# Four down row tiles behind the last product of a gate and up unit, in groups 2 to 6

## The chip, the core and the metric

The kernel runs on one core of a Trainium2 chip. The metric is the time of one execution on the device, in microseconds (us). Of the core's engines this case speaks of TensorE (PE, with its weight loads shown apart as PEld), VectorE (DVE), ScalarE (ACT), GpSimd (POOL), and SyncE (SP), which here issues DMAs only. GpSimd issues DMAs too, and does small adds.

## What is computed

The kernel computes a Fourier mixing layer, gated by a feed-forward layer, on x of 2048 rows and 448 columns in fp32:

```python
def _A_ref(x, dft_seq_re, dft_seq_im, dft_hid_re, dft_hid_im):
    a = jnp.einsum("bsd,ed->bse", x, dft_hid_re)
    b = jnp.einsum("bsd,ed->bse", x, dft_hid_im)
    y = jnp.einsum("ts,bse->bte", dft_seq_re, a) - jnp.einsum("ts,bse->bte", dft_seq_im, b)
    return y

def _B_ref(x, w_gate, w_up, w_down):
    return (_gelu(x @ w_gate) * (x @ w_up)) @ w_down

x = A_x
xn = _layernorm(x, axis=-1)
s = _A_ref(xn, A_dft_seq_re, A_dft_seq_im, A_dft_hid_re, A_dft_hid_im)
g = _silu(_B_ref(xn, B_w_gate, B_w_up, B_w_down))
return x + s * g
```

w_gate and w_up are 448 x 1792, w_down is 1792 x 448. The change lies in `_B_ref`.

## The kernel before

The 1792 feed-forward columns are 14 tiles of 128, taken in pairs: `GROUPS` has seven groups of two tiles, counted from 0. The 2048 rows are four chunks of 512. Group 0 computes gate and up directly. Groups 1 to 6 use a scheme with fewer products, in the function `strassen` (line 482): one call, a **unit**, makes gate and up for one tile of 128 columns and two chunks. A group has four units (tile 0 or 1, chunk pair 0 or 1), in the order of the loop at line 851; `gi` is the group, `bi` the unit in it, 0 to 3, and the text calls them first to fourth.

fp32 numbers are kept as a high and a low part, and a product is two or three matmuls of 128 x 128 weights against 512 columns (`three`, `two`, lines 470 and 477). A unit has 39 of them, in seven sums of 5 or 6 matmuls, in four accumulators in PSUM, `x1` to `x4`, in this order: x1, x2, x3, x4, then x1, x3 and x4 are opened again and added to. Between a first and a second filling another engine must have read the accumulator: ScalarE copies x1 (L500), VectorE adds x2, x3 and x4 into two temporaries (L505, L512, L516). After the second fillings ScalarE takes a GELU of x1 (L521), VectorE adds and multiplies (L525, L526), ScalarE writes the high part of the first product tile `hs` (L528), VectorE its low part (L530); then x4 is read (L534) and its GELU taken (L535). The unit's second product tile is finished in the next unit: L539 (VectorE, multiply), L541 (ScalarE, high part) and L544 (VectorE, low part) are passed on as `late` and called behind that unit's x1 and x2.

**Down** takes the product tiles of a group and a chunk and makes four row tiles of 128 rows (`down_one`, line 441): six matmuls of 448 columns into a PSUM tile `po`, then a ScalarE copy (L457) into a staging tile `po_out`. Behind the fourth copy GpSimd issues the DMA `gs<-po_out` (L462), which adds the staged tile to `gs` in device memory. The row tiles wait in a list, `dq`; `send` takes the next and emits it. `strassen` calls `dn[0]` to `dn[3]` at four places: behind x2, behind x4, behind the second filling of x3, and behind the second filling of x4. A unit in groups 2 to 6 emits four row tiles of work that earlier units made, one at each place.

Each engine takes its instructions in the order in which they are written; there is no scheduler. `preps` are steps of weight preparation that are written between the same places: a first and a fourth unit split the next weights (`prep_s`: ScalarE L356, VectorE L358 and L362), a third unit the down weights (`prep_d`: L384, L385), a second unit none. In groups 2 to 5 the second and the third unit begin with `sums_s` (line 332): ten GpSimd adds of 128 columns, L338 to L347, on the raw weights of the next group. They stand in GpSimd's queue behind the last unit's `gs` DMA, and in some units also behind two DMAs `sums<-ca` that `sum_step` issues there (L809).

Of the kernel before, what the change touches and what calls it, by code (L numbers as in the profile page):

```python
# [45 lines left out]
def fnet_geglu(ctx: ExitStack, tc: tile.TileContext, x, ca, ct, cp, et, wgu, wd, out):  # L46
# [209 lines left out]
    def t_places(p):  # L256
        if not t_lo:
            t_lo.append(sb.tile([P, 4096], FR, name="t_lo", tag="y"))
        h = [a_x[2 * p + 1][:, o : o + 512] for o in (0, 512, 2048, 2560)]
        l = [t_lo[0][:, 2048 * p + 512 * i :][:, :512] for i in range(4)]  # L260
        t_hl[p][0] = list(zip(h, l))

        def one(i):
            side, k = SPOT[i]
            split(h[i], l[i], xfk(2 * p + side, k))

        return one

    def v_places(p):
        v = sb.tile([P, 4096], FR, name=f"t_v{p}", tag=f"v{p}")  # L270
        vt[p] = v
        hl = []
        for side, k in SPOT:
            hl.append([v[:, 2048 * side + 512 * (k + 2 * a) :][:, :512] for a in range(2)])
        t_hl[p][1] = hl

        def one(i):
            side, k = SPOT[i]
            h, l = hl[i]
            n = 64 if i == 3 else P  # L280
            split(h[:n], l[:n], xfk(2 * p + side, k + 2)[:n])
            if i == 3:
                for a in (h, l):
                    nc.sync.dma_start(a[64:].bitcast(F32), a[:64].bitcast(F32))

        return one
# [12 lines left out]
    def load_s(f, i):  # L299
        raw = a_r[i]  # L300
        nc.sync.dma_start(raw[:, :1280], wgu[f].rearrange("p b f -> p (b f)"))
        return raw
# [29 lines left out]
    def sums_s(raw, eng):  # L332


        g2d, u2d, g3, u3, u0, g0, g1, u1, g2, u2, s3, s2, s4, s7, s6 = [
            raw[:, i * P : (i + 1) * P] for i in range(15)
        ]
        eng.tensor_sub(s3, g0, u0)  # L338
        eng.tensor_sub(s7, g2, u2)
        eng.tensor_add(u0, u0, u1)  # L340
        eng.tensor_add(u2[:64], u2[:64], u3[:64])
        eng.tensor_sub(s2, u0, g0)
        eng.tensor_sub(s6, u2, g2)
        eng.tensor_sub(s4, g1, s2)
        eng.tensor_sub(u2d, g2d, u2d)
        eng.tensor_add(u2d, u2d, g3)
        eng.tensor_sub(u2d, u2d, u3)  # L347
# [26 lines left out]
    def load_d(grp, at):  # L374
        rv = at[:, : 2 * D].rearrange("p (f d) -> p f d", f=2)
        nc.sync.dma_start(
            rv, wd[grp[0] * P : (grp[0] + 2) * P, :].rearrange("(f p) d -> p f d", p=P)
        )
        return rv
# [61 lines left out]
    def down_one(gi, c, wdn, kk):  # L441
        if gi > 0 and kk >= 2:
            po = tp_tile(f"po{gi}_{c}_{kk}")
        else:
            po = o_tile(f"po{gi}_{c}_{kk}")
        n = 0
        for i, f in enumerate(GROUPS[gi]):
            hs = hs_of[f, c]
            for a, b in ((0, 0), (0, 1), (1, 0)):
                nc.tensor.matmul(  # L450
                    po[:, :D], hs[:, a, kk * P : (kk + 1) * P], wdn[b][:, i],
                    start=n == 0, stop=n == 5,
                )
                n += 1
        if kk == 0:
            out_[0] = stage(c)
        nc.scalar.activation(out_[0][:, kk], po[:, :D], AF.Copy)  # L457
        if kk == 3:
            if gi == 0:
                nc.sync.dma_start(gv[:, 4 * c : 4 * c + 4], out_[0])  # L460
            else:
                nc.gpsimd.dma_start(gv[:, 4 * c : 4 * c + 4], out_[0], accum_op=ALU.add)  # L462
# [88 lines left out]
    with tc.manual_schedule():  # L551
# [156 lines left out]
        def fetch(p):  # L708
            nc.sync.dma_start(x_half(p), xp[p])
# [105 lines left out]
        def send():  # L815
            if dq:
                down_one(*dq.pop(0))

        nop = lambda: None
# [3 lines left out]
        def e_load(b):  # L823
            e_raw[b] = a_r[0][:, 960 * (b % 2) :][:, : 2 * D]
            nc.sync.dma_start(e_raw[b], et[b].rearrange("p r d -> p (r d)"))
# [17 lines left out]
        for gi in range(1, len(GROUPS)):  # L843
            grp = GROUPS[gi]
            nxt = GROUPS[gi + 1] if gi + 1 < len(GROUPS) else None
            ws = nws
            if gi > 1:
                wdn = nwdn
            nws, n_raw = [None, None], {}
            sides = (0, 0, 1, 1) if gi % 2 else (1, 1, 0, 0)  # L850
            for bi, (i, p) in enumerate(zip((0, 1, 1, 0), sides)):
                preps = [[], [], [], []]
                if gi == 1 and bi == 0:
                    tsp, vsp = t_places(1), v_places(1)
                    preps[0].append(lambda: (comb1.pop(0)(), vsp(3)))
                    preps[2].append(lambda: comb1.pop(0)())
                    preps[3].append(lambda: comb1.pop(0)())
                if gi == 1 and bi == 1:
                    comb1.pop(0)()
                    for n, f, k in ((0, vsp, 1), (1, tsp, 1), (2, tsp, 2), (3, vsp, 2), (3, tsp, 0)):  # L860
                        preps[n].append(lambda f=f, k=k: f(k))
                if gi == 1 and bi == 2:
                    vsp(0)
                    tsp(3)
                if bi == 0:
                    if gi == 1:
                        sums_s(s_raw2, nc.gpsimd)
                        n_raw[-1] = s_raw2
                    else:
                        n_raw[-1] = last_raw  # L870
                    ws[1], steps = prep_s(nw, n_raw[-1])
                    preps[1].append(steps[0])
                    preps[2].append(steps[1])
                    if nxt and gi > 1:
                        n_raw[0] = load_s(nxt[0], 0)
                    elif not nxt:
                        e_load(0)
                        e_load(1)
                elif bi == 1:
                    if nxt:  # L880
                        n_raw[1] = load_s(nxt[1], 1)
                        if gi > 1:
                            n_raw["d"] = load_d(nxt, a_s)
                            sums_s(n_raw[0], nc.gpsimd)
                        else:
                            wdn, steps = prep_d(grp, draw)
                            preps[1] += steps
                    else:
                        E_IN[0] = sb.tile([P, 1920], FR, name="e0", tag="r1")
                        preps[1].append(lambda: (e_split(0, E_IN[0]), e_load(2)))  # L890
                elif bi == 2:
                    if nxt:
                        if gi == 1:
                            n_raw["d"] = load_d(nxt, a_s)
                            n_raw[0] = load_s(nxt[0], 0)
                            sums_s(n_raw[0], nc.gpsimd)
                        sums_s(n_raw[1], nc.gpsimd)
                        nwdn, steps = prep_d(nxt, n_raw["d"])
                        preps[1].append(steps[0])
                        preps[2].append(steps[1])  # L900
                    else:
                        fetch(1)
                        E_IN[1] = sb.tile([P, 4 * D], FR, name="e1", tag="d1")
                        E_IN[2] = sb.tile([P, 2240], FR, name="e2", tag="sp")
                        preps[1].append(lambda: (e_split(1, E_IN[1]), e_load(3)))
                        preps[3].append(lambda: e_split(2, E_IN[2]))
                else:
                    if nxt:
                        nws[0], steps = prep_s(nw, n_raw[0])
                        preps[1].append(steps[0])  # L910
                        preps[2].append(steps[1])
                    else:
                        preps[1].append(lambda: e_split(3, vt[1][:, 7 * D :]))
                dn = [send] * 4
                if gi == 1 and bi < 2:
                    dn = [nop, send, nop, send]
                run = [lambda q=q: [f() for f in q] for q in preps]
                late = strassen(grp[i], p, ws[i], late, dn, run)
                sum_step(4 * gi + bi - 4)
                if bi % 2:  # L920
                    dq += [(gi, c, wdn, kk) for c in (2 * p, 2 * p + 1) for kk in range(4)]
            nw = 1 - nw
            if nxt:
                last_raw = n_raw[1]
# [484 lines left out]
```

## Time and profile before

| | us |
|---|---|
| Median of 3 runs | 769.03 (768.9 to 769.06) |
| The profiled execution | 769.27 |
| Its span in the trace | 767.5 |
| PE busy | 761.3 |
| DVE busy | 544.4 |
| ACT busy | 366.6 |
| POOL busy | 179.9 |

The span is what the trace covers from first to last instruction; the execution is 1.8 us longer. Times in rows are us from the span's start. In the chain of work that ended last, a row is a stretch of one engine and line; the chain's places are up to 0.2 us later than the start of the same matmuls in the timeline, since a row of a matmul overlaps the next. Groups 2 to 6 run from 122 to 398 us.

### The profile page before, as it was taken

The numbers are of one execution on the slowest core, as the hardware profiler recorded it, in microseconds if no ns is written. First come the engines' busy times: TensorE is split into PE (matmuls) and PEld (weight loads), VectorE is DVE, ScalarE is ACT, GpSimd is POOL, SyncE is SP. The second block draws the span as 40 slices with busy tenths as digits, with TensorE's granted clock in tenths as the row PEclk, the third lists the DMA queues.
The fourth block names the chain that finished last, engine by engine and source line by source line (L and its number), as shares of the span: only waits on it lengthen the run. The fifth ranks groups of instructions, "written<-read, shape, count | busy, mean of one in ns | idle before, by whom it ended". The sixth has DMA issues, their size and how long they took to land.

```text
span 767.5 us, 11360 instructions
## 1 busy us (share of the span) xinstructions
PE 761.3 (99%) x4054; PEld 686.2 (89%) x4054; DVE 544.4 (71%) x946; ACT 366.6 (48%) x547; POOL 179.9 (23%) x303
## 2 busy tenths in 40 slices
PE   8999999999999999999999999999999999999998
PEld 7988888888888888888889999999999999999997
DVE  7879877555556556455452777978888797979787
ACT  5975554444444344344444585534444444434341
POOL 2204043430501511501011001223222222323130
PEclk9999999999999999999999999999999999999999
DMA  8234458994959968774979981959696969688794
GB/s 298 91 120 150 145 203 172 263 186 104 266 107 252 272 117 225 172 157 84 257 218 240 372 346 54 325 170 334 210 354 205 346 202 343 211 304 268 256 312 153
DMA packets 61513, 170.04 MB, mean 222 GB/s; under 512 B 7440, under 2 KB 40080, under 8 KB 60560
## 3 DMA queue, kind: packets, MB, share of 16 engines
q0 software_dynamic: 13728, 61.02, 35.0%
q1 hardware_dynamic: 34272, 82.48, 30.5%
q10 hardware_dynamic: 13456, 25.81, 9.2%
q8 instruction: 32, 0.52, 0.3%
q14 instruction: 25, 0.20, 0.1%
HBM read 127.21 MB, written 70.91 MB: 258 GB/s over the span
## 4 chain that ended last, share of the span: by engine, by line
PE 99%; DVE 0%; issue 0%; DVEq 0%
PE x L473 24%; PE p L1173 22%; PE po L450 18%; PE p L1176 10%; PE ab L984 9%; PE x L480 4%; PE gu L396 4%; PE py L1188 1%; PE py L1190 1%; PE py L1189 1%; PE gu L599 1%; PE pt L198 1%; PE warm L573 1%; PE p L1206 0%; PE gu L585 0%
## 5 line engine op out<-in xcount | busy, mean ns | idle before, releaser
L473 PE MATMUL x<-xt,w 128*128 128x512 f32 x480 | 149.6, 392 | 0.0
L473 PEld LDWEIGHTS x<-xt,w 128*128 128x128 f32 x480 | 90.1, 188 | 16.3 <-DVE tmp L512 0.7
L457 ACT ACTIVATE po_out<-po 128x448 f32<-128x448 f32 x112 | 60.2, 537 | 81.7 <-PE po L450 79.5
L450 PE MATMUL po<-wd0h,hs 128*128 128x448 f32 x256 | 81.7, 366 | 0.0
L462 POOL DMA_DIRECT2D gs<-po_out x24 | 21.4, 893 | 218.7 <-ACT po_out L457 213.7
L984 PE MATMUL ab<-e,xt 128*128 128x448 f32 x288 | 68.8, 365 | 0.0
L450 PE MATMUL po<-wd,hs 128*128 128x448 f32 x288 | 66.0, 365 | 0.0
L473 PE MATMUL x<-t_v,w 128*128 128x512 f32 x216 | 60.8, 390 | 0.0
L450 PEld LDWEIGHTS po<-wd,hs 128*128 128x128 f32 x288 | 54.1, 188 | 6.7
L984 PEld LDWEIGHTS ab<-e,xt 128*128 128x128 f32 x288 | 54.1, 188 | 4.3
L450 PEld LDWEIGHTS po<-wd0h,hs 128*128 128x128 f32 x256 | 48.1, 188 | 4.9
L473 PEld LDWEIGHTS x<-t_v,w 128*128 128x128 f32 x216 | 40.6, 188 | 8.7
L1064 POOL DMA_DIRECT2D raw<-sums x45 | 24.8, 552 | 94.9 <-DVE xt L143 56.6
L450 PE MATMUL po<-wd0l,hs 128*128 128x448 f32 x128 | 46.9, 367 | 0.0
L142 ACT ACTIVATE e<-raw 128x896 fp32r<-128x896 f32 (+1 forms) x30 | 27.6, 921 | 38.6 <-DVE raw L1071 27.8
L528 ACT ACTIVATE hs<-tmp 128x512 fp32r<-128x512 f32 x24 | 15.2, 634 | 54.6 <-DVE tmp L526 54.6
L473 PE MATMUL x<-t_lo,w 128*128 128x512 f32 x96 | 37.4, 389 | 0.0
L142 ACT ACTIVATE e<-tmp 128x896 fp32r<-128x896 f32 (+1 forms) x22 | 19.7, 896 | 35.7 <-DVE tmp L1071 28.6
L1173 PE MATMUL p<-t_v,wd0l 128*128 128x448 f32 x112 | 36.4, 374 | 0.0
L1173 PE MATMUL p<-w,e 128*128 128x448 f32 x112 | 36.4, 374 | 0.0
L1064 POOL DMA_DIRECT2D tmp<-sums x39 | 21.5, 552 | 59.9 <-DVE xt L143 37.2
L358 DVE TENSOR_TENSOR w<-raw,w 128x512 fp32r<-128x512 f32 (+1 forms) x24 | 21.3, 888 | 18.3 <-ACT w L356 18.3
(374 smaller groups left out, 2017.6 us busy)
## 6 DMA issues: line engine op xcount, KB each, us to landing
gs<-po_out POOLq DMA_DIRECT2D x24, 896.0 KB, 7.8
sums<-ca SPq DMA_DIRECT2D x16, 896.0 KB, 11.2
sums<-ca POOLq DMA_DIRECT2D x16, 896.0 KB, 14.5
t_v<-td ACTq DMA_DIRECT2D x24, 448.0 KB, 5.8
w<-td ACTq DMA_DIRECT2D x24, 448.0 KB, 7.5
raw<-ct SPq DMA_DIRECT2D x45, 192.0 KB, 4.2
raw<-wgu SPq DMA_DIRECT2D x12, 640.0 KB, 5.9
tmp<-ct SPq DMA_DIRECT2D x39, 192.0 KB, 4.6
```

The source lines that it names most:

```text
L142: nc.scalar.activation(h, src, AF.Copy)
L358: nc.vector.tensor_sub(w[:, 1408 + lo : 1408 + b], raw[:, P + lo : P + b], hw[:, lo:b].bitcast(F32))
L396: nc.tensor.matmul(ps[:, cols], a, xt[:, cols], start=n == 0, stop=n == len(mm) - 1)
L450: nc.tensor.matmul(po[:, :D], hs[:, a, kk * P : (kk + 1) * P], wdn[b][:, i], start=n == 0, stop=n == 5,)
L457: nc.scalar.activation(out_[0][:, kk], po[:, :D], AF.Copy)
L462: nc.gpsimd.dma_start(gv[:, 4 * c : 4 * c + 4], out_[0], accum_op=ALU.add)
L473: nc.tensor.matmul(ps, a[i], b[j], start=first and n == 0, stop=n == 2, skip_group_check=True)
L480: nc.tensor.matmul(ps, a[0], xt, start=False, stop=True, skip_group_check=True)
L984: nc.tensor.matmul(p[:, :D], a, b, start=n == 0, stop=n == len(mm) - 1)
L1064: nc.gpsimd.dma_start(v[:, 4 * P : 6 * P], sums[j][:, KS.index(k)])
L1173: nc.tensor.matmul(ps[q][:, :D], h, v, start=u % UN == 0, stop=False, skip_group_check=True)
L1176: nc.tensor.matmul(ps[q][:, :HD], l, v[:, :HD], start=False, stop=u % UN == NS - 1, skip_group_check=True,)
```

## The change

The list of calls `dn` is filled differently. In group 1 nothing changes. In groups 2 to 6 the first three places are empty, and the fourth, behind the second filling of x4, emits four row tiles in a row.

```diff
-                dn = [send] * 4
-                if gi == 1 and bi < 2:
-                    dn = [nop, send, nop, send]
+                dn = [nop, nop, nop, lambda: [send() for _ in range(4)]]
+                if gi == 1:
+                    dn = [nop, send, nop, send] if bi < 2 else [send] * 4
```

The same row tiles are emitted in the same units, with the same matmuls, copies and DMAs. The order on GpSimd and SyncE is the same as before; on PE, ACT and DVE it moves, on DVE only in the numbers of the names.

On PE in the first unit of group 2, from the last products of x3's first filling to its second filling, before (the names are out<-in; `x3_4_1` is accumulator x3 of column tile 4 and chunk pair 1, `po1_2_1` a down row tile of group 1, `w` the weights, `xt`, `t_lo` and `t_v` parts of the input):

```order
L473 MATMUL x3_4_1_1252<-t_v1_822,w_73 128x512 x3
L473 MATMUL x4_4_1_1260<-xt3_69,w_73 128x512
L473 MATMUL x4_4_1_1260<-t_lo_728,w_73 128x512
L473 MATMUL x4_4_1_1260<-xt3_69,w_73 128x512
L473 MATMUL x4_4_1_1260<-t_v1_822,w_73 128x512 x3
L450 MATMUL po1_2_1_1271<-wd1_78,hs1_80 128x448 x3
L450 MATMUL po1_2_1_1271<-wd1_78,hs0_79 128x448 x3
L473 MATMUL x1_4_1_1225<-xt2_68,w_73 128x512 x3
L480 MATMUL x1_4_1_1225<-xt2_68,w_73 128x512 x2
L473 MATMUL x3_4_1_1252<-xt3_69,w_73 128x512
```

The same place now:

```order
L473 MATMUL x3_4_1_1244<-t_v1_822,w_73 128x512 x3
L473 MATMUL x4_4_1_1252<-xt3_69,w_73 128x512
L473 MATMUL x4_4_1_1252<-t_lo_728,w_73 128x512
L473 MATMUL x4_4_1_1252<-xt3_69,w_73 128x512
L473 MATMUL x4_4_1_1252<-t_v1_822,w_73 128x512 x3
L473 MATMUL x1_4_1_1225<-xt2_68,w_73 128x512 x3
L480 MATMUL x1_4_1_1225<-xt2_68,w_73 128x512 x2
L473 MATMUL x3_4_1_1244<-xt3_69,w_73 128x512
```

The six matmuls of a down tile that stood between the two fillings of x3 have left; so have those between x2 and x3, and those between the second fillings of x3 and x4.

On ACT at the end of the same unit, `hs` being the product tile, `tmp` the temporaries and `po_out` the staging tile (one piece of the difference):

```order
 L528 ACTIVATE hs_80<-tmp 128x512
-L457 ACTIVATE po_out<-po_2_2_1295 128x448
-L535 ACTIVATE tmp<-tmp 128x512
+L535 ACTIVATE tmp<-tmp 128x512
+L457 ACTIVATE po_out<-po_2_0_1287 128x448
+L457 ACTIVATE po_out<-po_2_1_1295 128x448
+L457 ACTIVATE po_out<-po_2_2_1303 128x448
 L457 ACTIVATE po_out<-po_2_3_1311 128x448
 L500 ACTIVATE tmp<-x_5_1_1332 128x512
 L541 ACTIVATE hs_79<-tmp 128x512
```

All four copies now stand in a row behind the second GELU (L535), ahead of the next unit's L500 and L541.

## Rows read from the trace of the kernel before

**Rows 1.** The chain that ended last, by engine, as shares of the span:

```profile
PE 99%; DVE 0%; issue 0%; DVEq 0%
```

**Rows 2.** Waits of PEld, 60 to 410 us: total us, times, longest:

```profile
PEld x L473 <- DVE tmp L512: 0.7, 2, 0.4
```

**Rows 3.** The chain in order of time: start us, us, what:

```profile
71.78 5.44 PE x L473 x24
...
122.36 2.74 PE x L473 x12
...
397.83 4.46 PE ab L984 x22
402.29 4.86 PE po L450 x24
```

**Rows 4.** Timeline, group 3's third unit: start, us, engine, line, out<-in [idle before]:

```profile
204.84 1.77 PE L473 MATMUL x<-xt,w 128*128 128x512 f32 x7
...
205.51 0.53 ACT L457 ACTIVATE po_out<-po 128x448 f32<-128x448 f32 x1
...
206.44 0.90 POOL L462 DMA_DIRECT2D gs<-po_out  x1 [5.44 <-ACT po_out L457]
...
207.50 0.76 POOL L339 TENSOR_TENSOR raw<-raw 128x128 f32<-128x128 f32 x1
...
210.01 0.72 POOL L345 TENSOR_TENSOR raw<-raw 128x128 f32<-128x128 f32 x1
...
208.46 2.84 DVE L544 TENSOR_TENSOR hs<-tmp,hs 128x512 fp32r<-128x512 f32 x1
211.22 0.67 DVE L512 TENSOR_TENSOR tmp<-tmp,x 128x512 f32<-128x512 f32 x1
```

**Rows 5.** Timeline of DVE, third unit of group 4:

```profile
263.55 2.82 DVE L544 TENSOR_TENSOR hs<-tmp,hs 128x512 fp32r<-128x512 f32 x1
```

**Rows 6.** Timeline, fourth unit of group 1:

```profile
116.62 0.67 DVE L512 TENSOR_TENSOR tmp<-tmp,x 128x512 f32<-128x512 f32 x1
...
116.89 0.62 PE L480 MATMUL x<-xt,w 128*128 128x512 f32 x2
...
117.35 0.19 PEld L473 LDWEIGHTS x<-xt,w 128*128 128x128 f32 x1 [0.28 <-DVE tmp L512]
...
117.69 0.39 PE L473 MATMUL x<-t_lo,w 128*128 128x512 f32 x1
```

**Rows 7.** Timeline, first and (201.46) second unit of group 3:

```profile
186.35 0.39 PE L473 MATMUL x<-xt,w 128*128 128x512 f32 x1
...
186.56 0.60 ACT L521 ACTIVATE tmp<-x 128x512 f32<-128x512 f32 x1 [0.61 <-PE x L480]
...
193.00 0.53 ACT L457 ACTIVATE po_out<-po 128x448 f32<-128x448 f32 x1
193.43 0.59 ACT L500 ACTIVATE tmp<-x 128x512 f32<-128x512 f32 x1
...
193.93 0.87 POOL L462 DMA_DIRECT2D gs<-po_out  x1 [12.90 <-ACT po_out L457]
...
201.46 0.69 DVE L525 TENSOR_TENSOR tmp<-tmp,x 128x512 f32<-128x512 f32 x1 [2.81 <-PE x L480]
```

**Rows 8.** Timeline, third unit of group 2:

```profile
149.75 1.09 PE L473 MATMUL x<-xt,w 128*128 128x512 f32 x4
...
151.30 0.88 POOL L462 DMA_DIRECT2D gs<-po_out  x1 [6.67 <-ACT po_out L457]
151.89 2.03 POOL L809 DMA_DIRECT2D sums<-ca  x2
...
153.36 0.69 DVE L544 TENSOR_TENSOR hs<-tmp,hs 128x512 fp32r<-128x512 f32 x1
```

**Rows 9.** Timeline, fourth unit of group 1:

```profile
112.72 0.47 POOL L339 TENSOR_TENSOR raw<-raw 128x128 f32<-128x128 f32 x1
...
112.78 0.95 DVE L539 TENSOR_TENSOR tmp<-tmp 128x512 f32<-128x512 f32 x1 [0.70 <-ACT tmp L535]
```

## What the change was expected to do

> **What bounds the kernel now.** I read the chain that ended last first: matmuls make up 99% of it [rows 1]. So a change gains only if it shortens the matmul stream, and loses only if it makes that stream wait. Next I read the waits of the matmul side from 60 to 410 us, where gate and up run. There are two, 0.7 us together, both of a weight load for L512, the vector add that reads the third sum [rows 2]; both lie in group 1, which the change leaves alone. From 122.36 to 397.83 us [rows 3] the chain holds twenty units, those of groups 2 to 6, and nothing but matmuls: 275.47 / 20 = 13.77 us each. These twenty units are the ones that are reordered. I call the start of a unit's first product zero and give all places as us after it.
>
> **The part that gains: fewer returns from down to the products.** A unit has 39 matmuls of 512 columns and 24 of 448. In a stretch without down tiles 24 of the wide ones take 5.44 us [rows 3], 0.2267 each; 24 narrow ones in a row take 4.86 us [rows 3]. So a unit should last 39 x 0.2267 + 4.86 = 13.70 us, and lasts 13.77. The rest, 0.073 us, I put on the four places where the stream comes back from down to the products: 0.018 us each. The change leaves one of the four, so a unit would take 13.72 us, and twenty units save 20 x 3 x 0.018 = 1.1 us. From below it is 0, if the rest has another cause; from above 20 x 0.073 = 1.5 us.
>
> **The part that can cost: the cover of the two adds.** With the down tiles gone from between them, the products stand back to back. The third sum is complete at 0.02 + 18 x 0.2267 = 4.10 and is opened again at 0.02 + 29 x 0.2267 = 6.59, with six products of the fourth and five of the first between. Before, twelve down matmuls (2.4 us) stood there as well. By then L512 must have read the third sum, and 1.13 us later L516 the fourth. Of the two only L512 is close: L516 is one add further, and has those 1.13 us for it. A late L512 holds a weight load of TensorE, and behind that the whole matmul stream. Ahead of L512 on VectorE stands L544, the low half of the previous unit's second product tile; it starts at 208.46 - 204.84 = 3.62 [rows 4], and the change does not move that, as it hangs on the second product alone. It takes 0.69 us as a rule [rows 8], so L512 starts as soon as the third sum is there, near 4.3, ends near 5.0, and has 1.5 us to spare. That holds in the first and fourth units of every group and in all of group 6.
>
> In the second and third units of groups 2 to 5 it need not hold, since there GpSimd runs ten small adds (L338 to L347). In the third unit of group 3 L544 took 2.84 us instead of 0.69: it ended at 211.30, just after L345 at 210.73, and L512 ended at 211.89 [rows 4]. Group 4 shows the same, 2.82 us [rows 5]. VectorE waited out the whole run of GpSimd adds up to L345. Before, this is free: down covers it. Now it is not. How long TensorE stands for a late L512 is seen in the fourth unit of group 1, where VectorE was late in spite of the cover: L512 ended at 116.62 + 0.67 = 117.29, two products that began at 116.89 put the next at 117.34 and its follower at 117.57, and the follower came at 117.69 [rows 6]. So the stream runs as if that product had begun 0.17 us behind the end of L512.
>
> **When GpSimd starts its adds after the change.** They stand in its queue behind the DMA of the staged down tiles, which waits for the copy of the fourth tile (L457), so the move of the down tiles moves them. From the last row of copy to the DMA's issue it is 193.93 - 193.00 = 0.93 us, and from the issue to the end of L512, when L544 is caught, 211.89 - 206.44 = 5.45 us [rows 4, 7].
>
> End of a first unit: the reopened first sum is complete at 6.59, its GELU (L521) starts 0.21 us later (186.56 against the next product at 186.35), and from there ScalarE and VectorE work as a closed chain up to the first copy that stands behind the second GELU, 193.00 - 186.56 = 6.44 us [rows 7]. So the first of the four copies is at 6.59 + 0.21 + 6.44 = 13.24, and at 0.43 us each (193.43 - 193.00) the fourth at 14.53. The unit ends at 13.72, so the DMA is issued at 14.53 + 0.93 - 13.72 = 1.74 of the second unit; before it was 1.1 us later, and L544 came ahead of the adds. Now L544 stands 3.62 - 1.74 = 1.88 us behind the issue, where the two caught ones stood 2.02. I take it as caught. L512 then ends at 1.74 + 5.45 = 7.19, the stream is back at 7.36 instead of 6.59: 0.77 us. This is so where only that DMA is ahead of the adds, in groups 2, 4 and 5: 3 x 0.77 = 2.3 us. In group 3 two DMA issues of the sums (L809) stand between, and hold GpSimd until 2.6 us behind the first issue (151.30 to 153.92 [rows 8]), at 4.36: L544 passes ahead of them and nothing waits.
>
> End of a second unit: it has no weight preparation, and from L525 (201.46) to the first copy behind the GELU (205.51) it is 4.05 us [rows 4, 7]. The reopened third sum is complete at 7.72, so the first copy would be at 11.96, the fourth at 13.25; but its products end with the unit, so it comes 0.21 us behind that end, and the issue at 1.14 of the third unit. In groups 3 and 4, where no L809 is ahead, L544 is caught as before, a little earlier: L512 ends at 6.59, the stream is back at 6.76, 0.17 us late, 0.3 us for both. In groups 2 and 5 L809 is ahead and holds GpSimd until 1.14 + 2.62 = 3.76; L544 starts 0.14 us before that, and I let it pass.
>
> The other moves are covered. The copies, L541 and the weight preparation have TensorE's down stretch of 4.9 us beside them (without it, a copy would cost its 0.43 us); loads that wait for raw weights to be read go out earlier on the sync queue; the staging buffer is written later than before, so the DMA that reads it has more time.
>
> **The sum.** -1.1 + 2.3 + 0.3 = +1.5 us. The profiled execution took 769.27 us, 0.24 above the median of 769.03; on the median the forecast is 770.5. Its own range, with the gain between 0 and 1.5 and the stall of a second unit between 0.6 and 0.9, is 769.6 to 772.0.
>
> **Rivals.**
>
> *The port is handed over between two adds.* In group 1 L539, begun at 112.78, ran 0.95 us while L339 ended at 113.19: it lost one add, not a run [rows 9]. If L544 gets in so in the second units, their 2.3 us are gone: 768.2. L339 ends 207.50 + 0.76 - 206.44 = 1.82 us behind the issue [rows 4], and L544 is to come at 1.88, so fourth copies 0.1 us later than reckoned would do. If it gets in everywhere, the 0.3 go too: 767.9. For it speaks the narrow 0.06 us; against it [rows 4, 5].
>
> The Trainium skill (SBUF — State Buffer, "Who interferes with whom") says that a VectorE instruction with two SBUF inputs contends with GpSimd's reads and that the second to issue blocks until the first finishes, that is one instruction. By that rule L544 would lose one add of 0.4 us and the time would be 767.9; the 2.84 us of rows 4 do not agree with one instruction, the 0.95 us of rows 9 do.
>
> *L544 is caught in the third units of groups 2 and 5 too*, clearly slower. Before, L544 began there at 153.36 - 149.75 = 3.61 with L809 held until 153.92, and took 0.69 us [rows 8]; the change shrinks that lead to 0.14 us. It decides if L544 comes over 0.14 us later, or if GpSimd takes the port at the end of L809's work. In rows 4 the DMA's work ends at 206.44 + 0.90 and the run 3.4 us later, and L512 another 1.16 after that. From 3.76 this puts the end of L512 at 8.3, the stream back at 8.5: 1.9 us in each, 772.4 with one and 774.3 with both.
>
> *The returns cost nothing*, and the rest per unit is only how products are spaced: then the stalls stand alone, 771.6.
>
> **Chances.** Forecast 0.55 (returns that cost nothing included, they lie in its range), port handed over 0.28, of it 0.1 everywhere, third units caught 0.12, something unseen 0.05. The range takes in 767.9 below and one caught third unit above: 767.8 to 772.5. A measurement of this kernel tells 0.2% from no change, 1.5 us, that is 767.5 to 770.6. The forecast sits at the upper edge, so half of its chance is slower: 0.28 + 0.12 + 0.03 = 0.43. No change: 0.27 + 0.25 = 0.52. Faster, 0.05, needs more than all four returns.
>
> **What would show it.** Units of 13.72 us in the chain where no adds run; weight loads that wait for L512 in the second units of groups 2, 4 and 5 (0.7 us each) and, short, in the third of 3 and 4; L544 rows of 2.8 us in those five; the staged DMA's issue at 1.7 of second units. It is wrong if L544 keeps 0.7 us there, if L809's units show a long one, or if a wait for ScalarE or for L516 appears.

## The result, and the profile after

The changed kernel takes 771.1 us (median; 770.91 to 771.36) where the kernel before took 769.08 (768.88 to 769.22): a ratio of 1.0025, 95% interval 1.0016 to 1.0035. It is slower, by 2.0 us; the forecast was 770.5 in a range of 767.8 to 772.5. The profiled execution is 771.36 us with a span of 769.5, against 769.27 and 767.5.

What the page of the kernel after says of the engines: busy us, share of the span, instructions, and under it the granted clock in 40 slices.

```profile
PE 762.7 (99%) x4054; PEld 686.4 (89%) x4054; DVE 551.9 (72%) x946; ACT 364.2 (47%) x547; POOL 179.7 (23%) x303
PEclk9999999999999999999999999999999999999999
```

The matmul stream is still the bound. Its granted clock is the upper of the two levels (2.4 GHz) all along, 0.999 of it in this execution and in the one before. The waits of the weight loads from 120 to 402 us, total us, times, longest; this is where [rows 2] had none:

```profile
PEld x L473 <- DVE tmp L512: 3.2, 5, 0.9
```

Five waits, all for L512. The chain of the kernel after (start us, us, what) tells where they are; the row that begins a unit is the one of 27 or of 12 products behind 24 down matmuls:

```profile
122.54 6.14 PE x L473 x27
...
136.26 2.76 PE x L473 x12
...
150.68 6.15 PE x L473 x27
...
205.62 6.15 PE x L473 x27
...
219.54 6.15 PE x L473 x27
...
247.01 2.76 PE x L473 x12
...
261.54 6.15 PE x L473 x27
...
275.48 6.15 PE x L473 x27
...
302.95 2.76 PE x L473 x12
...
317.45 6.15 PE x L473 x27
...
344.92 6.15 PE x L473 x27
...
399.85 2.23 PE ab L984 x11
```

From 344.92 to 399.85 stand four units with no adds beside them: 54.93 / 4 = 13.733 us each, against 13.774 [rows 3]. That is the gain, 0.041 us a unit, 0.82 us for twenty. Five units are longer than 13.733. The second of group 2 lasts 150.68 - 136.26 = 14.42 (0.69 more), the third of group 3 13.92 (0.19), the second and third of group 4 14.53 (0.80) and 13.94 (0.21), the second of group 5 14.50 (0.77): 2.66 us together. 2.66 - 0.82 = 1.84 us for groups 2 to 6. (The five waits add up to more, 3.2 us; what counts for the time is by how much the units grew.) The remaining 0.18 of the longer span lies ahead of them (122.54 against 122.36 [rows 3]), where the code is the same. Over the profiles of all the kernels here, that place varies from 122.10 to 122.54, so these 0.18 us are not shown to belong to the change.

The timeline of the kernel after in the second unit of group 2 shows one of the five (start us, us, engine, line, operation, out<-in, idle time before and its releaser):

```profile
135.62 1.83 ACT L457 ACTIVATE po_out<-po 128x448 f32<-128x448 f32 x4
...
136.10 1.78 PE L473 MATMUL x<-xt,w 128*128 128x512 f32 x7
...
137.80 0.88 POOL L462 DMA_DIRECT2D gs<-po_out  x1 [11.39 <-ACT po_out L457]
...
138.37 0.79 POOL L338 TENSOR_TENSOR raw<-raw 128x128 f32<-128x128 f32 x1
...
139.72 2.88 DVE L544 TENSOR_TENSOR hs<-tmp,hs 128x512 fp32r<-128x512 f32 x1
...
141.34 0.71 POOL L345 TENSOR_TENSOR raw<-raw 128x128 f32<-128x128 f32 x1
...
142.53 0.67 DVE L512 TENSOR_TENSOR tmp<-tmp,x 128x512 f32<-128x512 f32 x1
...
143.25 0.19 PEld L473 LDWEIGHTS x<-xt,w 128*128 128x128 f32 x1 [0.81 <-DVE tmp L512]
```

The four copies stand in a row, the DMA of the staged tiles goes out behind them at 1.70 of the unit, GpSimd's adds follow, and L544 (2.88 us instead of 0.69) ends only 0.55 us behind L345. L512 is queued behind it, and the weight load waits for L512. The third unit of group 3, which [rows 4] show from before, has the same picture. The DMA is issued earlier in the unit, so L544 begins later in the run of adds (2.48 us behind the issue, against 1.92 above), and the wait is shorter:

```profile
206.60 0.90 POOL L462 DMA_DIRECT2D gs<-po_out  x1 [6.09 <-ACT po_out L457]
...
209.08 2.37 DVE L544 TENSOR_TENSOR hs<-tmp,hs 128x512 fp32r<-128x512 f32 x1
...
212.10 0.19 PEld L473 LDWEIGHTS x<-xt,w 128*128 128x128 f32 x1 [0.30 <-DVE tmp L512]
```

And in the third unit of group 2, where L809 stands ahead of the adds, the counterpart of [rows 8], nothing is held:

```profile
152.21 2.02 POOL L809 DMA_DIRECT2D sums<-ca  x2
...
154.14 0.68 DVE L544 TENSOR_TENSOR hs<-tmp,hs 128x512 fp32r<-128x512 f32 x1
```

### The profile page after: what moved, and what is told of

Read it like the earlier page. It is cut to its first block, busy times and chain, and to the rows that moved or that the text cites. A ratio compares the mean times of both kernels' runs of the same rounds, so it can differ in the third digit from the quotient of the medians.

```text
span 769.5 us, 11360 instructions
## 1 busy us (share of the span) xinstructions
PE 762.7 (99%) x4054; PEld 686.4 (89%) x4054; DVE 551.9 (72%) x946; ACT 364.2 (47%) x547; POOL 179.7 (23%) x303
## 4 chain that ended last, share of the span: by engine, by line
PE 97%; issue 1%; DVE 1%; DVEq 0%
PE x L473 22%; PE p L1173 22%; PE po L450 18%; PE p L1176 10%; PE ab L984 9%; PE x L480 4%; PE gu L396 4%; PE py L1188 1%; PE py L1190 1%; PE py L1189 1%; PE gu L599 1%; PE pt L198 1%; PE warm L573 1%; PE p L1206 0%; DVE tmp L505 0%
## 5 line engine op out<-in xcount | busy, mean ns | idle before, releaser
L450 PE MATMUL po<-wd0h,hs 128*128 128x448 f32 x256 | 77.0, 367 | 0.0
L457 ACT ACTIVATE po_out<-po 128x448 f32<-128x448 f32 x112 | 54.9, 540 | 13.5 <-PE po L450 12.9
L450 PE MATMUL po<-wd,hs 128*128 128x448 f32 x288 | 61.3, 365 | 0.0
L505 DVE TENSOR_TENSOR tmp<-tmp,x 128x512 f32<-128x512 f32 x24 | 16.5, 688 | 61.7 <-PE x L473 61.3
L521 ACT ACTIVATE tmp<-x 128x512 f32<-128x512 f32 x24 | 14.4, 598 | 66.0 <-PE x L480 66.0
```

The source lines that it names most:

```text
L450: nc.tensor.matmul(po[:, :D], hs[:, a, kk * P : (kk + 1) * P], wdn[b][:, i], start=n == 0, stop=n == 5,)
L505: nc.vector.tensor_add(u, m, x2)
```

## The experiments

Two questions. Is the loss L544 alone, held by the run of adds, or do the bare products wait for something else too? And is the gain the price of returns from down to the products? Each kernel below is the changed kernel with one edit, unless it says otherwise. Times are medians beside runs of the kernel before on the same chip. That kernel took 769.26 us beside L544 moved, the changed kernel without the adds, two memsets, and four tiles behind x4; 769.12 beside one memset, the other order of the adds, two places, and four tiles behind x4 without the adds; 769.29 beside three places and the kernel before without the adds.

### L544 behind the fourth sum's add

```diff
         nc.vector.tensor_add(u, m, x2)
-        late[1]()
+        if f < 4:
+            late[1]()
...
         nc.vector.tensor_add(m, m, x4)
+        if f >= 4:
+            late[1]()
```

> The changed kernel, but in groups 2 to 6 the low half of the previous unit's second product tile (L544) is written behind L516 instead of ahead of L512. Theory (VectorE's L512 is late because L544 ahead of it waits out a run of GpSimd adds): the waits of weight loads for L512 fall from 3.8 us to the 0.6 us of group 1, L544 rows may still be long, and the time is 771.1 - 2.7 = 768.4 us (768.2 to 768.7). Rival (L512 itself, or TensorE, is slowed by the GpSimd adds, whatever stands ahead): the waits stay, 771.1. Rival (the gain from fewer returns is not real): waits gone, but 769.1 or more.

Measured: 768.47 us, ratio 0.999 (0.9981 to 0.9998). From 120 us on no weight load waits for L512's counterpart. In the five units that stalled, the moved instruction (L547 in this kernel) now comes at the end of the run of adds and takes 0.78 to 0.87 us. In the units with L809 it still meets the run, in the timeline of the second unit of group 3 for instance:

```profile
196.41 0.69 DVE L517 TENSOR_TENSOR tmp<-tmp,x 128x512 f32<-128x512 f32 x1 [0.67 <-PE x L473]
...
197.02 2.03 DVE L547 TENSOR_TENSOR hs<-tmp,hs 128x512 fp32r<-128x512 f32 x1
```

There the run of adds holds it, but the two instructions that release accumulators are now ahead of it. L513, which is what L512 was, runs beside the adds and is not late (at 140.12 for 0.69 us in the second unit of group 2). So the loss is the order on VectorE, L512 behind L544, and not the adds by themselves.

### Without the adds, after and before

The ten adds of the second and third units of groups 2 to 5 are left out, so the products of the next group have wrong weights.

```diff
-                            sums_s(n_raw[0], nc.gpsimd)
...
-                        sums_s(n_raw[1], nc.gpsimd)
+                            sums_s(n_raw[1], nc.gpsimd)
```

> The changed kernel without the ten GpSimd adds of the second and third units of groups 2 to 5, so that the weights of groups 3 to 6 are wrong; all else is as in the changed kernel. Theory: no L544 row over 0.7 us from group 2 on, no wait for L512 there, every unit 13.73 us: 768.4 us, the same as with L544 behind L516. Rival (the stalls come from the crowding of ScalarE's copies at the unit's end, not from GpSimd): 771.1. What is left against the 769.08 of the kernel before is the price of the returns from down to the products alone: forecast -1.1, from the profile of the changed kernel -0.8.

Measured: 768.26 us, ratio 0.9987 (0.9978 to 0.9996). The instructions of L544 from 88 to 398 us, shortest, median and longest ns:

```profile
L544 DVE TENSOR_TENSOR hs<-tmp,hs x24: 684/684/703, 88.3 to 397.9; 128x512 fp32r<-128x512 f32 x24
```

No long one is left, and no weight load waits in groups 2 to 6. The same edit in the kernel before asks whether the adds cost anything there:

> The kernel before without the ten GpSimd adds of the second and third units of groups 2 to 5 (the weights of groups 3 to 6 are wrong). Theory (before the change the adds cost nothing, since down tiles cover the late L512): units of 13.774 us everywhere and the time of the kernel before, 769.1 us within 0.2. Rival (the adds slow the kernel before too, and part of what the runs without adds gained is that): 768.3 to 768.7.

Measured: 769.18 us, ratio 0.9997 (0.9988 to 1.0006). The whole loss is made of adds that cost nothing before, because down covered them. The gain is there when they are gone, 0.9 us (769.18 - 768.26, from two chips).

### The adds later, by one and by two memsets

```diff
+        spot = const.tile([P, 104], F32, name="spot")
+
+        def hold():
+            for _ in range(2):
+                nc.gpsimd.memset(spot, 0.0)
...
+                            hold()
                             sums_s(n_raw[0], nc.gpsimd)
...
+                        else:
+                            hold()
                         sums_s(n_raw[1], nc.gpsimd)
```

> The changed kernel with two GpSimd memsets of 128 x 104 ahead of the ten adds in the second and third units of groups 2 to 5, which start the adds some 0.3 to 0.6 us later. Theory (L544 is caught for a whole run only if it comes when the run is past its first two adds): in the second units of groups 2, 4 and 5 L544 comes at or ahead of the second add, keeps under 1.2 us, and the 0.7 to 0.8 us stalls go (-2.3 us); in the third units of groups 3 and 4 it is still caught, and each stall grows by the delay, from 0.2 to 0.5 to 0.8 us (+0.6 to +1.2). Together 769.4 to 770.0 us. Rival (any overlap of L544 with the run costs the whole rest of the run): all five stalls grow by the delay, 772.6 to 774. Rival (VectorE loses one add at most, and the long rows have another cause): no change, 771.1.

Measured: 768.43 us, ratio 0.9989 (0.998 to 0.9997): better than expected, since the third units were not caught either. The third unit of group 3 in the timeline of this kernel:

```profile
206.99 0.46 POOL L338 TENSOR_TENSOR raw<-raw 128x128 f32<-128x128 f32 x1
207.42 0.46 POOL L339 TENSOR_TENSOR raw<-raw 128x128 f32<-128x128 f32 x1
...
208.15 0.70 DVE L544 TENSOR_TENSOR hs<-tmp,hs 128x512 fp32r<-128x512 f32 x1
208.26 0.91 POOL L341 TENSOR_TENSOR raw<-raw 64x128 f32<-64x128 f32 x1
```

L544 begins 1.16 us behind the first add, while the third (L340) runs, and takes 0.70; it is the add L341 that waits. So "past the first two adds means caught", on which I had built the expectation, is not the rule. The next kernel has one memset instead of two:

```diff
         def hold():
-            for _ in range(2):
-                nc.gpsimd.memset(spot, 0.0)
+            nc.gpsimd.memset(spot, 0.0)
```

> The changed kernel with one memset of 128 x 104 instead of two ahead of the ten adds in the second and third units of groups 2 to 5: the adds start some 0.25 to 0.4 us later than in the changed kernel. With two memsets L544 got in everywhere, at the latest 1.16 us behind the start of L338; in the changed kernel it was caught at 1.29 us and more. Theory (a place in time decides, between 1.16 and 1.29 us behind the start of L338): in the second units L544 comes about 1.0 us behind L338 and gets in; in the third units of groups 3 and 4 it comes 1.4 to 1.6 us behind, is caught, and the stall there grows from 0.2 to 0.45 to 0.65 us. 769.3 to 769.7 us, two waits for L512 in groups 2 to 6. Rival (any instruction between the DMA's issue and the adds breaks up the run, so that VectorE gets the port at each add): all L544 rows under 1.2 us, no waits, 768.4. Rival (delay alone, always caught): 772 or more.

Measured: 771.59 us, ratio 1.0034 (1.0021 to 1.0047), a second miss. All five units stall, a little longer than with no memset. The waits of the weight loads from 120 to 415 us:

```profile
PEld x L473 <- DVE tmp L512: 3.8, 5, 1.0
```

And the second unit of group 4 in the timeline:

```profile
249.30 0.82 POOL L338 TENSOR_TENSOR raw<-raw 128x128 f32<-128x128 f32 x1
249.73 0.80 POOL L339 TENSOR_TENSOR raw<-raw 128x128 f32<-128x128 f32 x1
...
250.47 3.08 DVE L544 TENSOR_TENSOR hs<-tmp,hs 128x512 fp32r<-128x512 f32 x1
```

Here L544 begins 1.17 us behind the first add, the same place as 1.16 above, and is held until L345 is done. What differs is how the adds' rows lie. In the held case they are 0.7 to 0.8 us long and each begins 0.3 to 0.4 us before the one ahead ends; in the free case they are 0.46 long, one every 0.42, and hardly overlap. The place in time does not decide by itself. (The page calls spans on GpSimd rough; I compare them among themselves alone.)

### The adds in an order where half need the one before

```diff
+    def sums_d(raw, eng):
...
+        eng.tensor_sub(s3, g0, u0)
+        eng.tensor_add(u0, u0, u1)
+        eng.tensor_sub(s2, u0, g0)
+        eng.tensor_sub(s4, g1, s2)
+        eng.tensor_sub(s7, g2, u2)
+        eng.tensor_add(u2[:64], u2[:64], u3[:64])
+        eng.tensor_sub(s6, u2, g2)
+        eng.tensor_sub(u2d, g2d, u2d)
+        eng.tensor_add(u2d, u2d, g3)
+        eng.tensor_sub(u2d, u2d, u3)
...
-                            sums_s(n_raw[0], nc.gpsimd)
+                            sums_d(n_raw[0], nc.gpsimd)
```

The same ten adds; five of them need the result of the one just ahead, where two did. The call for the other tile is replaced in the same way, in groups 2 to 5 alone.

> The changed kernel with the ten GpSimd adds of the second and third units of groups 2 to 5 in another order, in which most adds need the result of the one just ahead (third on second, fourth on third, seventh on sixth, ninth on eighth, tenth on ninth). In the traces VectorE gets in at L345 to L346, where L346 needs the result of L345. Theory (a run holds the port as long as no add waits for the one just ahead of it): L544 loses 0.2 to 0.9 us instead of 2.2, no stall or one of up to 0.2 us in each place: 768.4 to 768.8 us. Rival (the ten adds hold the port as one run in whatever order): 771 us or more, waits for L512 as in the changed kernel.

Measured: 768.26 us, ratio 0.9988 (0.9979 to 0.9997). The timeline of this kernel in the second unit of group 2, where L559 is what L544 was and L353 to L362 are the adds:

```profile
138.18 0.80 POOL L353 TENSOR_TENSOR raw<-raw 128x128 f32<-128x128 f32 x1
139.06 0.46 POOL L354 TENSOR_TENSOR raw<-raw 128x128 f32<-128x128 f32 x1
139.60 0.94 POOL L355 TENSOR_TENSOR raw<-raw 128x128 f32<-128x128 f32 x1
...
139.54 0.68 DVE L559 TENSOR_TENSOR hs<-tmp,hs 128x512 fp32r<-128x512 f32 x1
```

L559 comes at 3.6 of the unit, in the run as in the changed kernel, and takes 0.68 us; the add that meets it (L355) waits instead. An instruction that is held waits for a gap in the run: in the changed kernel it is let in where L346 must wait for L345, and here five of the ten adds give such a place. This is shown for where it gets in. Why two memsets (and not one) had the same effect, the rows of the two alone do not say: they differ only in that the adds overlap or don't, and in group 1 of the kernel before an L544 was held though they did not (its timeline):

```profile
114.43 2.27 DVE L544 TENSOR_TENSOR hs<-tmp,hs 128x512 fp32r<-128x512 f32 x1
...
114.43 0.46 POOL L342 TENSOR_TENSOR raw<-raw 128x128 f32<-128x128 f32 x1
114.85 0.46 POOL L343 TENSOR_TENSOR raw<-raw 128x128 f32<-128x128 f32 x1
```

The other half is the place in the run. In the traces of all twelve kernels, from group 1 on, the VectorE instructions with two SBUF inputs that begin during these adds (in the order of the changed kernel) part without an exception. Where the rows do not overlap, 28 began before L341 and lost at most 0.33 us, and 27 began with L341 to L344 and lost 0.56 to 2.00. Where the rows overlap, the border lies earlier: 19 began with L338 (or with L339, where L809 stands ahead) and lost at most 0.33, and 37 began with L340 to L344 and lost 0.69 to 2.63. The L544 of group 1 begins with L342 and is held. So is L385 with two memsets, in the third unit of group 2, which begins with L343 (1.09 us is its usual time):

```profile
155.87 2.25 DVE L385 TENSOR_TENSOR wd<-xf,wd 128x896 fp32r<-128x896 f32 x1
...
155.87 0.45 POOL L343 TENSOR_TENSOR raw<-raw 128x128 f32<-128x128 f32 x1
```

So two memsets freed L544 by both: the adds no longer overlap, and it begins before L341. With one memset they overlap, and it begins behind the start of L340. Why the border lies there stays open.

### How many returns, and where

A unit with two places of two tiles, behind x4 and behind its second filling:

```diff
-                dn = [nop, nop, nop, lambda: [send() for _ in range(4)]]
+                dn = [nop, lambda: [send() for _ in range(2)]] * 2
```

> In groups 2 to 6 two down row tiles stand behind the first filling of x4 and two behind the last product: two returns from down to the products per unit instead of four (before) or one (the change). Theory (each return costs 0.0134 us, (13.7735 - 13.7333) / 3 from the two profiles): units of 13.747 us, 20 x 2 x 0.0134 = 0.54 us under the kernel before, 768.6 to 768.8 us against 769.2; no wait for L512, which has two down tiles, 2.4 us, of cover. Rival (the gain comes from the last place alone, the four tiles in a row): 769.2.

Measured: 768.31 us, ratio 0.9989 (0.9981 to 0.9998). And three places:

```diff
-                dn = [nop, nop, nop, lambda: [send() for _ in range(4)]]
+                dn = [nop, send, send, lambda: [send() for _ in range(2)]]
```

> In groups 2 to 6 one down row tile stands behind the first filling of x4, one behind the second filling of x3, two behind the last product: three returns from down to the products per unit. Units last 13.774 us with four returns, 13.734 with two (two row tiles and two) and 13.733 with one (four row tiles). Theory A (each return costs the same, and with 24 down matmuls ahead of it more than with 12): units of 13.754 us, 0.4 us under the kernel before. Theory B (what costs is to have single row tiles between the products at all, or the place behind x2): 13.735 to 13.745, 0.6 to 0.8 under. No wait for L512 in groups 2 to 6 in either.

Measured: 768.82 us, ratio 0.9995 (0.9986 to 1.0004). The chains of the two, the first row at the start of a unit of group 6 and the last at the group's end, three units later; first of two places, then of three:

```profile
355.61 5.45 PE x L473 x24
...
396.81 4.46 PE ab L984 x22
```

```profile
355.99 5.46 PE x L473 x24
...
397.25 4.46 PE ab L984 x22
```

With two returns a unit takes 41.20 / 3 = 13.733 us, with three 41.26 / 3 = 13.753. Four returns give 13.774 [rows 3] and one 13.733. So from four to three and from three to two the unit gains 0.02 us each time, about what was reckoned for a return; the last one that the change takes away is worth nothing that the chain shows. I had not expected two places to do as well as one. That the number of returns is what costs is not shown: one price for every return would give 13.747 and 13.760 us for two and three. Four, two, none and none of the returns of these kernels stand behind a single row tile, and 0.01 us for each of those fits all four times. No run here changes the single row tiles and leaves the number as it is.

With two and two, L544 is caught in the third units of groups 3 and 4 (3.27 and 3.26 us), and no weight load waits from group 2 on: twelve down matmuls, 2.43 us together, stand between the two fillings of x3.

### All four behind the first filling of x4

```diff
-                dn = [nop, nop, nop, lambda: [send() for _ in range(4)]]
+                dn = [nop, lambda: [send() for _ in range(4)], nop, nop]
```

> In groups 2 to 6 the four down row tiles stand together behind the first filling of x4 instead of behind the last product. One return from down to the products per unit as in the changed kernel, but 4.9 us of down between the first filling of x3 and its second. Theory: the gain stays (-0.8 against the kernel before) and no weight load waits for L512 in groups 2 to 6, even where L544 is caught: 768.3 us (768.0 to 768.7). Rival (putting the four tiles together is what costs, wherever they stand, by ScalarE's four copies in a row): 770 us or more, with waits for ScalarE.

Measured: 781.16 us, ratio 1.0165 (1.0145 to 1.0185), the largest miss. The cover of L512 and L516 is back, but the fourth copy, the DMA behind it and so the adds move ahead of the end of the unit that emits the tiles (in the first unit of group 2 the DMA is issued at 133.59, 11.3 us into the unit). The waits of the weight loads from 120 to 415 us:

```profile
PEld x L473 <- DVE tmp L534: 9.9, 8, 2.8
PEld x L473 <- DVE w L358: 4.1, 2, 2.1
```

Two instructions of VectorE behind these waits, from the timeline of group 2:

```profile
135.33 3.47 DVE L358 TENSOR_TENSOR w<-raw,w 128x896 fp32r<-128x896 f32 x1 [5.62 <-ACT w L356]
...
153.53 3.06 DVE L530 TENSOR_TENSOR hs<-tmp,hs 128x512 fp32r<-128x512 f32 x1 [0.70 <-ACT hs L528]
```

L358 (weights that the next unit needs) and L530 (ahead of L534, which releases the fourth accumulator for the next unit) meet the run now, and the down tiles that covered them are gone from the end of the unit. To see that nothing else is in it, the same kernel without the adds of the second and third units of groups 2 to 5:

> The four down row tiles behind the first filling of x4, as in the run that took 781.2 us, but without the ten GpSimd adds of the second and third units of groups 2 to 5 (the weights of groups 3 to 6 are wrong). In that run weight loads waited for L534 and L358, and L358 and L530 rows of 3.5 and 3.1 us stand in units with GpSimd adds, while fourth units and group 6 kept 13.73 us. Theory (those stalls too come from VectorE instructions caught by a run of adds, now L358 and L530, which stand uncovered between the products): 768.3 us, no waits. Rival (the chain from x1's and x3's second filling through the GELUs to the reading of x4 is too long without down tiles behind it): the waits for L534 stay, 775 us or more.

Measured: 768.29 us, ratio 0.9991 (0.9982 to 1.0): all of the 12.9 us is the adds.

## Why the prediction was right

**The bound and the places.** Right: five weight loads wait, in the second units of groups 2, 4 and 5 and the third of 3 and 4, and none elsewhere from group 2 on.

**When GpSimd starts.** The DMA of the staged tiles was forecast at 1.74 of a second unit and came at 137.80 - 136.10 = 1.70; in the third unit of group 3 forecast 1.14, and 206.60 less the unit's first product, at 205.45 in the timeline, is 1.15. This step, that the adds move because the copies move, carries the whole loss; the experiment behind x4 shows how much more it can cost. One reading in it was off: before the change, L544 did not come ahead of the adds in the second units of groups 2, 4 and 5. It began 0.17 to 0.23 us behind the start of L338 and lost only 0.10 to 0.16 us.

**The size of the stalls.** The second units were forecast at 0.77 each and cost 0.69, 0.80 and 0.77; the third at 0.17, and cost 0.19 and 0.21. Sum 2.66 against 2.6. L512 ended at 143.20 - 136.10 = 7.10 where 7.19 was expected. The cover is misread in one place, without effect on the sum: six down matmuls (1.21 us) stood between the two fillings of x3 before, not twelve; six more stood ahead of its first filling. From the unit's start to the reopening it is 2.4 us less all the same.

**The units with L809.** Right: L544 took 0.68 us in the third units of groups 2 and 5, and 0.83 in the second of 3. The rival that it is caught there falls. In the third unit of group 2 L809's work ends at 152.21 + 2.02 = 154.23 and L544 began at 154.14, a lead of 0.09 us where 0.14 was reckoned. That it was a near thing is not shown: no L544 in any run began between the end of L809 and L340 (at 155.20 there), and the held ones all began behind the start of L340.

**The gain: the mis-sized term.** Forecast 1.1 us, three returns of 0.018 each in twenty units; measured 0.82. The step that failed is the even split of the rest of 0.073 us over four returns. The three that left were worth 0.041 us a unit and not 0.055: two steps of 0.02, the third next to nothing, and 13.733 - 13.70 = 0.03 us of the rest stays with one return. That (0.3 us in all), the 0.18 us ahead of group 2 in one profiled execution, and 0.06 us more of stalls are what separates the sum of +1.5 from the span's +2.0.

**The port handed over between adds.** It did not happen in the changed kernel, in none of the five places. The margin of 0.06 us on which I had set its chance was not the point: with one memset the adds began 0.12 us later behind the DMA's issue, and L544 was held as before. In the changed kernel it began 0.40 to 0.48 us behind the start of L340 in the second units, and none of the instructions that began with L340 to L344 in such a run got in before L346. With two memsets, and with the adds in dependent order, L544 got in within one add in groups 2 to 5. By the Trainium skill (SBUF — State Buffer, "Who interferes with whom") the second to issue waits for the first instruction to finish; the 0.68 to 0.89 us of L544 in groups 2 to 5 of these two kernels agree with that, the 2.36 to 3.31 us of the held rows do not.

**A faster kernel.** The change is worth about 0.8 us once the run of adds is out of L512's way. The versions with L544 moved (768.47), the adds reordered (768.26), two memsets (768.43) and two places of two (768.31) are not told apart by the intervals of their ratios, and all of these lie below 1.

## What to carry to other kernels

Before work is taken from between two fillings of an accumulator, list every instruction that stands in the in-order queue ahead of the one that empties it, with its longest time in the trace and not its usual one: here an instruction that had been 2.84 us long at no cost came to hold TensorE. Moving work also moves what is queued behind it on other engines: the copies took a DMA with them, and the DMA the adds. And a move need not be whole: two row tiles at each of two places gave all of the gain here (13.733 us a unit) and kept the cover.

## What the runs showed of the hardware

- A run of GpSimd adds on SBUF can hold a VectorE instruction with two SBUF inputs until an add has to wait for the one ahead of it: 2.36 to 3.31 us instead of 0.69 for the L544 that were caught in groups 2 to 5. VectorE adds with one input in PSUM are not held: L517 took 0.69 us at 196.41 beside the run that held L547 for 2.03.
- Whether it is held went with the place in the run, in all traces: begun before the fourth add (the third, where the rows of the adds overlap) it lost at most 0.33 us, 47 times; begun from there to the seventh it lost 0.56 to 2.63, 64 times.
- The same adds in dependent order gave L544's counterpart its place within 0.15 us, and it was the add that lost 0.5 us (0.94 instead of 0.46).
- Two memsets ahead of the run freed L544 in all five places, one in none, with L544 at the same 1.16 and 1.17 us behind the first add. Two did not free L385, which began with the sixth add (2.25 us instead of 1.09).
- A unit took 13.774, 13.753, 13.733 and 13.733 us with four, three, two and one returns from 448-column to 512-column matmuls. Whether the number of returns or the single row tile ahead of one costs is not shown.
